# A long-convolution and mixer kernel: the matmuls of its last inverse stage put 16 apart, and its task order written out anew

## Chip, cores and metric

The kernel runs on one core of one Trainium2 chip, in one launch. The metric is the device time of an execution in microseconds (us), as the median of several runs. "Before" stands for the kernel without the change, "after" for the one with it.

## Reference

S = 2048 tokens, D = 640 channels, F = 1728. One sample, bfloat16 inputs. Cut to what matters:

```
mod = silu(c) @ w_mod                      # c is 1 x 640; six vectors sa, ca, ga, sb, cb, gb
q   = LN(x) * (1 + ca) + sa                # x = A_q
ks  = causal 4-tap convolution of k over the tokens, per channel
kv  = ks * v
y   = irfft(rfft(kv, 4096) * rfft(ssm_k, 4096))[:2048] + kv * ssm_D
x   = x + ga * (q * y)
h   = LN(x) * (1 + cb) + sb
g   = gelu(LN(h) @ w1)                     # 640 x 640
hs  = (g, its four quarters moved by +1, -1, +2, -2 tokens) @ w2
x1  = h + hs
h2  = gelu(LN(x1) @ w3) @ w4               # 640 x 1728, 1728 x 640
out = x + gb * (x1 + h2)
```

## The kernel before

**Tasks and their order.** The kernel builds 1056 numbered tasks with `add` (L91): for each a function that issues its instructions, the engines it may go to, what it reads and writes, and cost numbers. `run` (L121) then walks the string `ORDER` at the top of the file. A word such as `475P:20` is a task number, an engine letter (P TensorE, A ScalarE or ACT, D VectorE or DVE, G GpSimd or POOL, S SyncE or SP, which issues DMAs) and the PSUM places that the task takes, out of four places of two banks each. The functions are called in that order, so it fixes what each engine does one after the other, and on which engine a task with a choice lands. Within an engine nothing overtakes. The cost numbers are not read when the order is given.

**The convolution.** A transform of length 4096 is done as a product of small ones, 64 by 64. `to_slots` (L391) turns 32x32 blocks on DVE, `stage1` (L399, matmuls L408) and `stage2`/`stage2_half` (L416, L434; matmuls L425, L446) transform ssm_k and kv. ssm_D is added to the first tap of ssm_k (L461). `k_shift` (L472) does the four taps as matmuls with diagonal weights (L480). PSUM is read out by `evac` (L205; ACT is L208, DVE L210). `inverse1` (L623) multiplies the spectra on DVE (L633) and transforms back with matmuls L644 and L645, evacuated into the tile T01. `inverse2` (L673) is the last inverse stage: for tile A of 128 tokens it takes 32 matmuls (L685) of 32x32 weights (Hs) by 160 columns (Zb, in T01), one for each row group j4, column group cg and half cpp; the two halves of one j4 and cg add up in the same place of PSUM. It is called for the tile groups [0,1,2], [3,4], [5,6,7], [8,9,10], [11,12,13], [14,15]: the PE tasks 475, 478, 482, 485, 488, 491. Two evacuations of each (for 475: 476 and 477) write y_all.

**The modulation.** `mod_half` (L501) loads half of one of the six vectors' weights (400 KB), does five matmuls (L509) and stores a row of modv (L516 to L524). Tasks 428/429/430 and 431/432/433 are load, matmuls and evacuation of sb, 434 to 439 of gb. `x_load` (L538) brings x in pieces; 205 to 208 are the four pieces of its second half. `ln1_stats` (L549) and `make_q` (L613) make q; 444 and 447 are statistics of x tiles 11 and 13.

**The mixer.** `chain_a` (L756) forms q * y (L761) and adds it to x (L764); its tasks 520, 499, 540 are the first. `square_sum` (L752, ACT L753) and `ln_finish` (L720: a small first task on POOL or DVE, L726 to L731, and a second on POOL, L736 to L741) make the statistics of a layer norm. `chain_b` (L770; L775, L779, L780) makes h, `chain_c` (L808) normalizes it (`norm`, L605 to L610, or `normed`, L745) and transposes it with `turn` (L786): by PE and an evacuation (L796, L802/L804) for early groups, by a transposing DMA from SP (L789) for later ones. `mm_w1` (L831: L842 with gelu L844; L852 with gelu L858), `mm_w2` (L887: L897, evacuated by DVE at L904), `mm_w3` (L916: L931, gelu L935) and `mm_w4` (L939: L961, L952; DVE L984 to L990, stores L993) follow for groups of one or two tiles. The tasks 517, 536, 515, 556 are w1 of tiles 0, 1 and 2, 560/561 the first w2 and its evacuation, 600/598 w1 of the group of tiles 3 and 4, 649 to 652 normalization and transposing DMA of tiles 5 and 6, 661/659 their w1, 729 the L852 matmuls of tiles 7 and 8, fed by the transposing DMAs 718 and 720.

**Weights.** w1 (452) and w2 (453 to 457) are loaded into RG. w3 (494, L1020) and w4 (495 to 497) go where T01 was, so their loads wait until the last task of `inverse2` has read it.

Of the kernel before, what the change touches and what calls it, by code (L numbers as in the profile page):

```python
# [26 lines left out]
18D 19G 20D 21G 23D 24A 22D 27G 29D 36G 37G 30A 28D 50G 0S 2S 68G 69D 25A 31A 26G 84P:0 86P:1 88P:2 51D 53A 4S 72G 73D 106P:3 85A 87A 38G 104P:0 89A  # L27
107A 6S 3S 70G 71D 39G 40A 102P:1 103A 5S 74G 98P:2 99A 105D 8S 90P:3 91A 49G 118P:0 75D 110P:1 9S 119D 94P:2 32G 111A 95A 112P:3 113A 108P:0 109A
116P:1 114P:2 115A 1S 66D 67D 96P:3 117D 80P:0 82P:1 10S 122P:2 41G 42G 43G 44A 97A 52D 54A 45D 81A 83D 11S 123D 33G 78P:3 79A 100P:1 101D 76P:0 77A
136D 92P:2 34S 47S 120P:3 121D 93A 179P:1 55G 180A 46S 7S 193P:0 194A 35S 195P:2 196A 181P:1 147P:0 148A 182D 201S 141P:3 142D 139P:2 140A 143P:1  # L30
199P:0 175P:3 200A 48S 176A 144D 204S 185P:2 186D 161P:1 162A 65G 157P:0 158D 171P:3 172A 203S 165P:2 166D 191P:1 192A 167P:0 155P:3 156A 168D 169P:2
170A 177P:1 178D 189P:0 190A 151P:3 159P:2 160A 202S 152D 145P:1 146D 187P:0 188A 149P:3 150D 197P:2 198A 183P:1 184D 153P:0 154A 163P:3 164A 262P:2
173P:1 174A 12S 137P:0 138A 13S 214D 263A 126P:3 56G 264P:1 210D 254D 127D 57G 124P:0 125D 211D 58G 59G 60A 61G 62G 63G 265A 260P:2 215A 266P:1 267A
261A 14S 255D 64A 15S 128P:3 129D 258P:0 259A 270P:1 271A 130P:2 131D 256D 16S 212A 276P:0 277A 268P:1 269A 132P:3 134P:2 17S 133D 135D 257D 282P:0
209A 283A 223S 213G 224P:1 225A 220S 278P:3 226S 286P:2 287D 279A 221P:0 222A 272P:1 273A 274P:3 275A 227P:0 228D 469D 284P:1 463D 342S 285A 292P:2
293D 288P:0 289A 232S 233P:3 234D 290P:1 291D 466D 296P:2 297A 294P:0 295A 229S 230P:3 231D 343G 310P:1 302P:2 303A 311D 235S 460D 312P:3 313A 298P:0
299D 308P:1 309A 236P:2 237D 467D 300P:3 301A 306P:0 307D 280P:2 281A 316P:1 317D 252G 314P:3 315A 253S 304P:0 305D 318P:2 319A 248G 247G 320P:1 321A
241S 336P:3 340P:2 341A 337A 243G 240S 330P:0 331A 338P:1 339A 367G 251S 250G 239S 326P:2 322P:3 323A 464D 345D 344D 348P:0 349A 244G 346P:1 347A 352D
245S 249G 334P:3 238S 242S 351G 246G 335A 350S 353D 356P:0 357A 354P:1 366S 324P:3 325A 327D 359G 332P:2 333A 358S 360D 361D 362P:0 363A 368D 364P:3
328P:2 329A 355A 369D 370P:0 371A 365A 376D 375G 374S 372P:2 377D 378P:1 379A 380P:0 373A 381A 384D 217A 382S 383G 385D 388P:3 389A 391G 390S 393D  # L40
392D 386P:1 400D 387A 396P:2 397A 394P:0 398S 399G 401D 402P:3 425S 403A 404P:1 405A 408D 395A 426P:2 407G 406S 409D 416D 410P:3 415G 414S 417D 412P:1
431S 411A 465D 413A 461D 462D 427D 216G 420P:0 421D 418P:3 419A 470D 422S 423P:1 424D 471D 468D 218A 475P:20 476A 477D 520D 499D 434S 456S 500D 521D
540D 541D 543D 459G 472A 435P:3 436A 523D 473D 474D 432P:1 437S 438P:2 219G 501A 433A 512A 478P:03 439A 522A 502G 503G 428S 429P:1 430A 504D 505D 542A
491P:21 525D 479A 524G 507D 526D 528D 492A 506A 480A 568D 527A 545D 485P:02 487A 493A 486A 206S 544G 546D 547A 207S 508G 509D 510P:3 529G 511A 530D
531P:2 532A 482P:10 481G 569D 570A 548D 452S 571D 572D 574D 573A 458G 517P:3 518A 205S 513D 536P:2 533D 484D 549G 483A 550D 534D 575G 580D 581D 576D
455S 582D 457S 577D 578D 208S 514D 538P:3 584D 537A 535D 634D 635D 631D 539A 583A 488P:01 551P:2 552A 579A 585G 586D 515P:3 589D 632D 449D 489A 558P:2
516A 637D 559A 556P:0 557A 636A 453S 587P:3 633A 638G 590P:2 591A 490A 497S 588D 454S 560P:0 561D 562A 643D 600P:2 601A 639D 494S 563G 564G 598P:3
599A 498G 640D 641D 565D 566P:1 602P:0 605P:2 642A 644D 645D 647D 646A 648G 441D 649D 650S 567A 618P:3 446A 616P:1 603D 604A 651D 652S 620P:0 553A
496S 619A 606D 661P:2 617A 443D 607A 440D 608G 609G 613D 659P:3 610D 622P:1 444D 621A 554D 555D 699D 700D 662A 660A 614P:0 615A 611P:2 666P:3 667D
663P:0 612A 683P:2 623A 442G 664D 701A 668A 684A 665A 669G 670G 671A 679P:1 680A 677P:3 495S 674D 672P:0 675P:2 678A 592D 593D 595D 596D 597D 673A  # L50
594D 702D 624P:1 676A 749P:3 765D 766D 703D 704A 681P:0 747P:2 750A 682A 445G 653D 654D 655D 768D 769D 770A 705G 706G 625D 626D 767A 745P:3 685P:10
748A 743P:2 771G 707D 708D 711D 709D 710A 686P 712D 713D 772G 773D 777A 715G 714A 716G 717A 718S 774D 778D 779D 780A 775D 776A 744A 781D 719D 720S
687D 746A 447D 782G 783A 785D 448G 729P:1 730A 786S 727P:2 728A 784S 795P:3 721A 656D 693D 796A 657D 658D 831D 628S 832D 793P:0 450D 694D 724A 451G
722D 734P:1 723D 794A 834D 835D 836A 697S 787D 735D 731P:2 732D 737D 797P:3 798D 833A 751P:01 696S 688D 837G 838G 843D 800P:2 736A 725D 752P 844D 845D
733A 738G 741D 689S 839A 840D 841D 739A 801D 803D 627S 799A 847D 802A 740S 842A 846A 742S 753D 811P:3 812A 804G 807D 805A 815P:2 788D 809P:0 848G 851D
816A 813P:3 810A 849D 726D 852S 850S 855P:2 856A 808S 790D 853P:0 806S 873P:2 759D 854A 860P:1 791D 792D 891D 892D 789D 951D 952D 954D 857P:0 894D
895D 629S 893A 814A 861D 897D 896A 630S 898G 899D 900D 858D 863D 692S 875P:3 876A 871P:1 869P:3 691S 872A 754D 757S 870A 695S 817P:01 901D 874A
877P:32 818P 862A 859A 864G 903D 819D 758S 904D 905D 906A 865D 867D 868S 866S 907D 902A 908G 909D 911D 953A 955G 956D 957D 935P:0 936A 958D 960G 959A
961G 878P 690S 760D 825D 756S 912S 755S 519G 962D 826D 885D 910S 915P:0 916A 913P:1 914A 698S 820D 879D 931P:0 762S 963S 966P:2 967A 964P:1 917P:3
918D 920P:2 921D 822S 965A 969P:1 970D 932A 968G 1003P:0 933P:3 929P:2 827S 828S 919A 922A 923G 924G 927D 928S 764S 925D 926S 1004D 1005A 972P:1 973D  # L60
934A 971A 930A 937P:03 987P:2 761S 988A 981P:1 983P:2 763S 880D 884S 883S 824S 823S 821S 886D 887S 890S 939D 975D 974A 976G 985P:0 977A 979D 889S 982A
829S 938P 945D 882S 984A 978S 986A 980S 1016P:1 1014P:2 1010P:0 1017A 1011A 881S 1015A 1012P:3 1006G 1007G 1008D 1009S 989P:10 1013A 946D 830S 940D
941S 991D 947S 1032P:2 888S 992D 993S 996S 943S 1038P:3 990P 997D 1036P:1 1033A 1042D 1037A 1018P:20 995S 949S 1034P:1 1035A 1019P 944S 942S 998D
1002S 1000S 999S 950S 1020D 948S 1021D 1023S 1025S 1026D 1039A 994S 1027D 1001S 1024S 1040P:21 1022S 1043D 1030S 1028S 1031S 1044D 1045D 1047S 1048S
1046S 1029S 1049S 1041P 1050D 1051D 1055A 1052S 1053A 1054S
# [72 lines left out]
def kernel(  # L138
# [16 lines left out]
    add = pl.add  # L155
# [5 lines left out]
    T01 = mem.tile([P, 20480], BF, name="T01")  # L161
    R3 = mem.tile([P, 20480], BF, name="R3")
    R5 = mem.tile([P, 20560], BF, name="R5")
    RG = mem.tile([P, 8192], BF, name="RG")
# [67 lines left out]
    for b in range(ND):  # L232
        for dst, off, src, key in ((kT, 16, k_flat, "kT"), (vT, 0, v_flat, "vT")):
            add("SP", 3.0, lambda e, b=b, dst=dst, off=off, src=src: nc.sync.dma_start_transpose(dst[:, b, off:off + S], src[:, b * P:(b + 1) * P]),
                w=[(key, b, b + 1)], kb=524, rate=200.0)
# [100 lines left out]
    for kb in range(2):  # L336
# [9 lines left out]
        else:  # L346
# [3 lines left out]
            r=[wk[:3]], w=[wk], port=0.4)  # L350
# [83 lines left out]
    def stage2_half(h):  # L434
        for k0 in range(0, 32, 3):
            kn = min(3, 32 - k0)
            ps = Slot()

            def f(e, ps=ps, k0=k0, kn=kn, hh=h + 2):
                psv = pst(ps, name="ps_s2")[:, :, 0:480].rearrange("p g (k s) -> p g k s", k=3)  # L440
                for j in range(kn):
                    k = k0 + j
                    for cc in range(2):
                        for g in range(2):
                            p = slice(64 * g, 64 * g + 64)
                            nc.tensor.matmul(psv[:, g, j], lhsT=Gs[p, k, 64 - 64 * cc:192 - 64 * cc], rhs=T1h[h][p, cc * 32 + k],  # L446
                                             start=(cc == 0), stop=(cc == 1), tile_position=(64 * g, 0))
            t0 = add("PE", 0.145 * kn, f, r=[("T01", 10240 * h, 10240 * h + 10240), ("RG", 192 * k0, 192 * (k0 + kn))], alloc=ps, ni=8 * kn)
# [224 lines left out]
    def inverse2(tilesA):  # L673
# [3 lines left out]
        def f(e):  # L677
            for s in pss:
                pst(s, name="ps_i2")
            for a, A in enumerate(tilesA):  # L680
                for j4 in range(4):
                    for cg in range(4):
                        n1 = 4 * A + cg
                        for cpp in range(2):
# [35 lines left out]
    def ln_finish(li, t0, n, quick):  # L720
# [21 lines left out]
        add("POOL", 1.0 if quick else 1.3, f, port=-1, r=[("s2", 100 * li + t0, 100 * li + t0 + n), ("nm" + k, 0, 1)], w=[("ln" + k, 0, 1)])  # L742
# [346 lines left out]
```

## Time and profile before

| what | value |
|---|---|
| median of 3 runs | 302.70 us (302.69 to 303.25) |
| the profiled execution | 302.69 us |
| its span | 301.0 us |
| TensorE granted clock, mean | 0.97 |
| busy: PE, weight load, DVE, ACT, POOL | 271.0, 207.3, 220.8, 204.4, 108.9 us |
| first and last PE instruction | 8.43 and 296.2 us after the span's start |

The profile is that of one execution, taken by the hardware. Its page gives each engine's busy time, the span in forty equal slices (a digit is the busy tenths of a slice; PEclk is the TensorE clock that was granted, 9 being full), the DMA queues, the chain of work that ended last, and the costliest groups of instructions as "line, engine, operation, out<-in". Further views are cut from the same trace: busy time in chosen stretches, the chain in order of time, the timeline of one engine (in brackets the idle time ahead of a row and what ended it), and waits. "issue" means idle time in which an engine waited for nothing that the profile shows. PEld is the weight load of TensorE.

### The profile page before, as it was taken

What the parts mean: (1) busy time and instruction counts of PE and PEld (TensorE: products, weight loads), DVE (VectorE), ACT (ScalarE), POOL (GpSimd) and SP (SyncE); (2) the same over time, 40 slices, a digit from 0 to 9 for tenths busy, and PEclk for the clock granted to TensorE, in tenths of its full rate; (3) what the DMA queues carried; (4) which work ended last, traced back from release to release, by engine and by line L of the source; (5) the groups of instructions that cost most, each with busy time, mean ns of one, the idle gap of its engine ahead of it and who ended that gap; (6) DMA issues with size and microseconds to landing.
All of it is one profiled execution on the core that took longest, in us unless ns stands there. A gap on an engine that the chain in (4) does not pass through costs nothing.

```text
span 301.0 us, 7658 instructions
## 1 busy us (share of the span) xinstructions
PE 271.0 (90%) x3054; PEld 207.3 (69%) x3054; DVE 220.8 (73%) x446; ACT 204.4 (68%) x345; POOL 108.9 (36%) x238
## 2 busy tenths in 40 slices
PE   0899999979989576878999999999999999999993
PEld 0665655758888345756888787688867887887771
DVE  7999999979999979998659969983547343231343
ACT  4798999979999869998864679646451642604110
POOL 4967641451256646242345534310125120300000
PEclk9999999999999955799999999999999999999999
DMA  5998999998899940352900040234014112310121
GB/s 180 272 221 189 200 195 234 235 201 215 224 258 293 257 107 2 108 208 44 293 6 1 2 93 14 54 68 43 18 23 93 40 29 60 75 30 19 46 54 45
DMA packets 58179, 35.75 MB, mean 119 GB/s; under 512 B 39872, under 2 KB 54848, under 8 KB 58144
## 3 DMA queue, kind: packets, MB, share of 16 engines
q1 hardware_dynamic: 56944, 31.88, 45.2%
q0 software_dynamic: 1104, 3.34, 4.2%
q8 instruction: 24, 0.39, 0.5%
q14 instruction: 11, 0.09, 0.1%
q10 hardware_dynamic: 96, 0.04, 0.1%
HBM read 16.31 MB, written 2.62 MB: 63 GB/s over the span
## 4 chain that ended last, share of the span: by engine, by line
PE 71%; ACT 11%; DVE 6%; DMA 6%; issue 3%; POOL 1%; SPq 0%; ACTq 0%; DVEq 0%; POOLq 0%
PE ps_w L931 19%; PE ps_w L961 19%; PE ps_w L897 6%; PE ps_ksh L480 6%; PE ps_s L408 6%; PE ps_w L842 4%; ACT T L208 4%; ACT R L208 3%; PE ps_s L425 2%; PE ps_mod L509 2%; DMA RH<-in_w_mod_dram 2%; DMA Ra<-in_A_ssm_k_dram 2%; DVE R L780 1%; PE ps_i L644 1%; PE ps_s L446 1%
## 5 line engine op out<-in xcount | busy, mean ns | idle before, releaser
L931 PE MATMUL ps_w<-R,T 128*128 128x256 bf16 (+1 forms) x630 | 64.0, 261 | 0.0
L931 PEld LDWEIGHTS <-T 128*128 128x128 bf16 x630 | 55.7, 98 | 7.2 <-issue 1.1
L961 PE MATMUL ps_w<-T,R 128*128 128x320 bf16 x416 | 59.2, 299 | 0.0
L935 ACT ACTIVATE R<-ps_w 128x1024 bf16<-128x1024 f32 (+2 forms) x36 | 29.1, 828 | 42.1 <-PE ps_w L931 42.1
L961 PEld LDWEIGHTS <-R 128*128 128x128 bf16 x416 | 40.2, 98 | 15.8 <-ACT R L935 0.3
L208 ACT CAST T<-ps_s 128x1024 bf16<-128x1024 f32 x34 | 32.7, 1023 | 1.1 <-PE ps_s L408 1.1
L984 DVE TENSOR_TENSOR T<-ps_w,R 128x640 bf16<-128x640 f32 x15 | 12.3, 823 | 27.3 <-PE ps_w L961 14.0
L408 PE MATMUL ps_s<-F1bd,Rb 128*128 128x256 bf16 x160 | 22.9, 294 | 8.4 <-DVE Rb L395 8.4
L753 ACT ACTIVATE RG<-R 128x640 bf16<-128x640 bf16 x32 | 23.6, 736 | 10.2 <-DVE R L904 7.1
L208 ACT CAST R<-ps_s 128x640 bf16<-128x640 f32 (+1 forms) x36 | 26.7, 828 | 2.8 <-PE ps_s L446 1.9
L738 POOL TENSOR_TENSOR lnv<-stat,lnv 128x2 f32<-128x2 f32 x19 | 4.9, 256 | 62.6 <-ACT RG L753 33.0
L408 PEld LDWEIGHTS <-Rb 128*128 128x128 bf16 x160 | 16.4, 105 | 14.7 <-DVE Rb L395 8.8
L904 DVE SCALAR_TENSOR_TENSOR R<-ps_w,R 128x640 bf16<-128x640 f32 x16 | 13.1, 821 | 14.5 <-PE ps_w L897 14.5
L739 POOL TENSOR_TENSOR lnv<-lnv,mhalf 128x2 f32<-128x2 f32 (+1 forms) x29 | 22.3, 770 | 2.3
L897 PE MATMUL ps_w<-RG,R 128*128 128x320 bf16 x160 | 23.1, 299 | 0.0
L842 PE MATMUL ps_w<-R,RG 128*128 128x256 bf16 (+1 forms) x200 | 21.0, 267 | 0.3 <-ACT Rb L208 0.3
L644 PE MATMUL ps_i<-EA,Rb 128*128 128x128 bf16 x160 | 19.1, 219 | 1.2 <-ACT T L208 0.4
L645 PE MATMUL ps_i<-EB,Rb 128*128 128x128 bf16 x160 | 19.0, 219 | 0.5 <-DVE Rb L633 0.5
L897 PEld LDWEIGHTS <-R 128*128 128x128 bf16 x160 | 15.4, 98 | 6.0 <-issue 0.3
L842 PEld LDWEIGHTS <-RG 128*128 128x128 bf16 x200 | 18.2, 107 | 1.7 <-issue 0.4
L480 PE MATMUL ps_ksh<-R,RQ 128*128 128x512 bf16 x80 | 18.8, 380 | 0.0
L858 ACT ACTIVATE R<-ps_w1x 32x256 bf16<-32x256 f32 (+1 forms) x40 | 13.2, 330 | 7.8 <-PE ps_w1x L852 7.5
(179 smaller groups left out, 524.3 us busy)
## 6 DMA issues: line engine op xcount, KB each, us to landing
Ra<-in_A_ssm_k_dram SPq DMA_DIRECT2D x5, 512.0 KB, 5.6
Ra<-in_A_q_dram SPq DMA_DIRECT2D x8, 320.0 KB, 6.7
R<-in_w_mod_dram SPq DMA_DIRECT2D x6, 400.0 KB, 6.3
out_dram<-RH SPq DMA_DIRECT2D x60, 40.0 KB, 1.6
T<-in_B_w_dram SPq DMA_DIRECT2D x1, 2160.0 KB, 8.5
T<-in_B_w_dram SPq DMA_DIRECT2D x1, 2080.0 KB, 9.5
RH<-in_w_mod_dram SPq DMA_DIRECT2D x4, 400.0 KB, 4.3
RK<-R POOLq DMA_DIRECT2D x5, 256.0 KB, 4.5
```

Source lines behind the costliest of these rows:

```text
L208: nc.scalar.copy(dst, src(ps.tile))
L408: nc.tensor.matmul(psv[:, ml, :], lhsT=xL[:, s0:s0 + P], rhs=F1r, start=True, stop=True)
L480: nc.tensor.matmul(pt[:, i, :], lhsT=diagw[:, b, jj, :], rhs=kT[:, b, c0:c0 + 512], start=(jj == 0), stop=(jj == 3))
L644: nc.tensor.matmul(psv[:, w, :], lhsT=Av[:, r_, :, g_], rhs=EAf, start=True, stop=False)
L645: nc.tensor.matmul(psv[:, w, :], lhsT=Bv[:, r_, :, g_], rhs=EBf, start=False, stop=True)
L739: nc.gpsimd.tensor_tensor(rs, rs, mhalf[:, 0:n], ALU.pow)
L753: add("ACT", 0.74, lambda e: nc.scalar.activation(junk, src, ACT.Square, scale=float(D) ** -0.5, accum_out=stat[:, li, 1, t:t + 1]), r=[sk ...
L842: nc.tensor.matmul(pt[:, fb, 0:cw], lhsT=w1_sb[:, b, 160 * fb:160 * fb + P], rhs=hT[:, b, 0:cw], start=(b == 0), stop=(b == ND - 1))
L897: nc.tensor.matmul(pt[:, hf, 0:320], lhsT=gsf[:, fb, c0:c0 + P], rhs=w2_sb[:, fb, 320 * hf:320 * hf + 320], start=(fb == 0), stop=(fb == 4))
L931: nc.tensor.matmul(pt[:, fl, 0:cw], lhsT=w3_sb[:, b, fb * P:(fb + 1) * P], rhs=xT[:, b, 0:cw], start=(b == 0), stop=(b == ND - 1))
L935: nc.scalar.activation(g3[g % 2][:, f0:f0 + fn, 0:cw], ps.tile[:, 0:fn, 0:cw], ACT.Gelu_apprx_tanh)
L961: nc.tensor.matmul(bank(i, hf), lhsT=gg[:, fb, i * P:(i + 1) * P], rhs=w4_sb[:, fb, 320 * hf:320 * hf + 320], start=(fb == 0 and i == 0), ...
```

## The change

Three things change.

1. The string `ORDER` is replaced as a whole. The PE tasks are the same 241. The tasks with a choice of engine change like this: evacuations (L206 to L210) 9 from ACT to DVE and 9 from DVE to ACT; normalizations (L606 to L610) 13 from DVE to ACT and 6 from ACT to DVE; evacuations of PE transposes (L799 to L804) 5 from ACT to DVE and 1 back; layer-norm statistics of x 2 from DVE to ACT and 1 back; the first task of `ln_finish` 7 from DVE to POOL and 4 from POOL to DVE; one L461 from POOL to DVE; DMA copies of the tables and half spectra 7 from SP to POOL and 4 from POOL to SP. Tasks in all: DVE 308 and then 302, ACT 249 and 253, POOL 99 and 104, SP 159 and 156. The cut below shows the part around the last inverse stage.
2. In `inverse2` the loop over the two halves, cpp, is moved outside the loops over j4 and cg. The two matmuls that add into one place of PSUM are 16 matmuls apart; they were neighbours.
3. Cost numbers of `stage2_half` and `ln_finish` change, and an unused default argument goes.

```diff
 ORDER = """
...
-431S 411A 465D 413A ... 218A 475P:20 476A 477D 520D 499D 434S 456S 500D 521D
-540D 541D 543D 459G 472A 435P:3 436A 523D 473D 474D 432P:1 437S 438P:2 219G 501A 433A 512A 478P:03 439A 522A 502G 503G 428S 429P:1 430A 504D 505D 542A
-491P:21 525D 479A 524G 507D 526D 528D 492A 506A 480A 568D 527A 545D 485P:02 ...
...
+427D 452S 410P:1 411A 412P:2 413A 420P:0 421D 418P:1 419A 422S 423P:3 456S 461D 470D 424D 468D 462D 218A 475P:20 477D 476A 520D 459G 454S 499D 500D
+471D 521D 472A 540D 434S 219G 523D 541D 543D 437S 438P:1 439A 512A 435P:3 428S 429P:2 430A 431S 432P:0 501A 522A 433A 436A 525D 502G 504D 457S 478P:12
+480A 503G 524G 526D 505D 473D 491P:03 545D 542A 544G 507D 553A 492A 527A 474D 546D 479A 571D 568D 485P:20 ...
...
 """
@@ stage2_half
-            def f(e, ps=ps, k0=k0, kn=kn, hh=h + 2):
+            def f(e, ps=ps, k0=k0, kn=kn):
...
-            t0 = add("PE", 0.145 * kn, f, ...
+            t0 = add("PE", 0.17 * kn, f, ...
@@ inverse2
             for a, A in enumerate(tilesA):
-                for j4 in range(4):
-                    for cg in range(4):
-                        n1 = 4 * A + cg
-                        for cpp in range(2):
+                for cpp in range(2):
+                    for j4 in range(4):
+                        for cg in range(4):
+                            n1 = 4 * A + cg
                             nc.tensor.matmul(pss[j4 // 2].tile[32 * cg:32 * cg + 32, j4 % 2, a * 160:(a + 1) * 160],
                                              lhsT=Hs[32 * j4:32 * j4 + 32, n1, cpp, :],
                                              rhs=Zb[32 * j4:32 * j4 + 32, cpp * 64 + n1, :, :],
                                              start=(cpp == 0), stop=(cpp == 1), tile_position=(32 * j4, 32 * cg))
@@ ln_finish
-        add("POOL", 1.0 if quick else 1.3, f, ...
+        add("POOL", 0.8 if quick else 1.1, f, ...
```

The loads that stand on SP's queue from 425 (w_mod) to 496 run, before: 425, 431, 422, 434, 456, 437, 428, 206, 207, 452, 205, 455, 457, 208, 453, 497, 454, 494, then the transposing DMAs 650 and 652, 496, 495. After: 425, 452, 422, 456, 454, 434, 437, 428, 431, 457, 208, 207, 453, 455, 206, 494, 205, 497, 652, 650, 495, 496.

## The prediction, made before the changed kernel was run

> **What bounds the kernel now.** I read the page first: the engines' shares, the forty slices, the chain. The profiled execution took 302.69 us, the median of the three runs is 302.70, so the sum below is made against 302.69 and stands for the median too. The span is 301.0; 1.69 us lie around it and I leave them alone. About 0.2% (0.6 us) is what a measurement of this kernel can tell from no change.
>
> ```profile
> span 301.0 us, 7658 instructions
> ...
> PE 271.0 (90%) x3054; PEld 207.3 (69%) x3054; DVE 220.8 (73%) x446; ACT 204.4 (68%) x345; POOL 108.9 (36%) x238
> ...
> PE   0899999979989576878999999999999999999993
> ...
> PEclk9999999999999955799999999999999999999999
> ```
>
> TensorE holds the end, but the PE row has a dent: slices 14 to 19 (about 98 to 143 us), and the granted clock falls there. So I asked for the busy time by stage, in stretches that begin where the final inverse stage begins and where PE is full for good:
>
> ```profile
> 60.00:98.20 38.20, 34.05 (x606) 29.53 (x605) 36.07 (x39) 35.66 (x43) 16.38 (x27) 1.00 0.94 238
> 98.20:143.13 44.93, 32.88 (x752) 25.07 (x753) 40.10 (x108) 39.74 (x88) 20.01 (x51) 0.81 0.44 120
> 143.13:296.30 153.17, 153.09 (x1318) 120.64 (x1318) 87.53 (x214) 76.36 (x140) 38.62 (x105) 1.00 0.24 53
> ```
>
> Columns after the length: busy PE, weight load, DVE, ACT, POOL, clock, DMA share, GB/s. From 143.13 PE is busy 153.09 of 153.17 us: nothing but its own sum counts. From 98.20 to 143.13 PE is idle 12 us, DVE and ACT are busy 40.1 and 39.7 of 44.9: they bound that stretch, by the order in which they take their tasks. The chain of waits there:
>
> ```profile
> 98.20 1.20 PE ps_i L685 x88
> 99.40 2.14 PE ps_mod L509 x15
> 101.54 0.55 PE ps_i L685 x22
> 102.09 3.70 issue
> 105.79 0.97 PE ps_i L685 x41
> 106.76 1.46 PE ps_mod L509 x5
> 108.24 0.43 ACT modv L524
> 108.77 0.90 DVE R L780 x2
> ...
> 140.39 2.60 DMA R<-RK
> 143.00 0.14 issue
> 143.13 0.71 PE ps_w1x L852 x5
> ```
>
> Two things are to be seen. First, PE stops for 3.70 us at 102.09 inside the second L685 task, with nothing to wait for ("issue"). The trace's records of the queue "instruction" (24 fetches of 16 KB, one for each 256 PE instructions) say why: fetches began at 91.09 and 102.89 us, after 1785 and 2241 PE instructions had started, 456 apart where 240 to 310 is usual. The late one took 1.30 us; PE went on 1.6 us after it. The loads issued from 93.3 to 98.7 (w_mod, x, w1, w2) keep all DMA engines full at 220 to 370 GB/s just then. Second, 429, the mod row queued behind that task on PE, comes 3.7 us late, and DVE waits for it:
>
> ```profile
> 108.77 0.89 DVE L780 SCALAR_TENSOR_TENSOR R<-R,lnv,modv 128x640 bf16<-128x640 bf16 x1 [1.74 <-ACT modv L524]
> ```
>
> So the point that sets the end is X, the start of task 661 (143.13 now): the time after is X plus PE's remaining sum (153.1) plus the tail (4.8).
>
> **Part 2, the inner order of L685.** Nothing is added: 512 matmuls and 512 weight loads as before. The timeline shows task 475 (96 matmuls, three tiles) from 98.20 to 99.33, 0.376 us a tile at full clock: 16 tiles, 6.0 us. Bounds: at most the stream itself, 160 columns at the 2.35 columns per ns of L931's 128x256 (109 ns apart) over 16 array positions and 32 matmuls, 0.14 us a tile; the quickest 32 matmuls of the trace took 0.21 us. So the stage may lose 0 to 2.6 us of PE time (3.8 at the extreme), but PE has 12 us of idle time here, and only 475 is waited for directly (its evacuations 476 and 477 start chain_a): at most 3 x 0.17 = 0.5 us. The other way, if 16 open accumulations were dearer than neighbours, nothing in the trace excludes +0.5. I take -0.2 on the path. Of the fetch stall it takes nothing: a quicker task runs dry sooner and waits for the same fetch.
>
> One rule speaks against this part. "TensorE: Matmul & The Clock Gate" in the Trainium skill, Part 3, "The mechanism", says that a weight load overlaps matmuls in flight only when its row group differs. The new order still takes four column groups of one row group in a row, and by that rule three of four loads stay unoverlapped and the gain is nothing: the sum would be 0.2 us worse.
>
> **Part 3, cost numbers and an unused default.** They feed no instruction: the order is read from the string. 0.
>
> **Part 1, the order.** PE has the same 241 tasks; 60-odd tasks elsewhere change engine (18 evacuations and 19 normalizations among them). I summed each engine's old durations along the new order.
>
> *To 60 us:* DVE's running sums stay within 0.2 us at the first transposes and PE's order is nearly the same; the k and v transposes for block 4 come before 2. 0. *To 98.2:* ACT's tasks ahead of 476 sum to 99.08 instead of 98.40 us (+0.68), PE's wait at 60.65 for w_mod has 0.44 more PE work ahead of it. ACT is 93% busy there, so I put chain_a 0.9 later (row 520: 100.78 to 101.65). **+0.9, less the 0.2 above.**
>
> *Mod rows.* The new order records all four of that time (438, 435, 429, 432) right after 475, ahead of the second L685 task. Their loads, by the same rates and the new queue order, land at 96.5 to 101.5, and all four lie before instruction 2241. The fetch stall stays (I estimate 105.2 plus or minus 1, against 105.79, since the same loads are in flight) but what is behind it now are L685 tiles that DVE needs only later. **-1.74** on DVE and -2.67 on ACT (its wait on L509). If cover is gone (a mod load lands 3 us later), they come back in full.
>
> *DVE to the first w2 evacuation (561).* From 520 to 561 DVE's own tasks sum to 24.96 before and 24.19 after, -0.77: seven small statistics tasks go to POOL. Each such pair of rows occupies DVE for 0.3 to 0.4 us with its gaps (104.59 to 105.22 for two), not the 0.2 its durations say: -0.77 to -1.9, I take **-1.2**. POOL is busy 20 of 45 us here and has room; its rows are about 0.26 us (L738), and where a normalization waits for them (L741: 0.46, 0.28, 0.65) the waits grow, up to +0.5 each for the three; I take **+0.3**. So 561 starts at 131.13 + 0.7 - 1.74 - 1.2 + 0.3, about 129.2.
>
> *From there to X.* The last normalization before the transposing DMA ends at 140.05 now. After: task 444 (1.1 us, x statistics) and 563 (0.33) go ahead, one L904 (0.82) goes behind: +0.6; the wait of 0.65 ahead of 138.50 is filled by 444: -0.65; 0.28 at 132.24 partly: -0.2. Two transposes in the other sequence and the 2.60 of the DMA are unchanged. **-0.2.** Sum at X: 0.7 - 1.74 - 1.2 + 0.3 - 0.2 = -2.1; ACT's tasks up to there are +0.26 in sum, against its -2.67, so it doesn't take over. X about 141.0.
>
> *The full tail.* PE's sum after X is the same, but PE takes 729 (w1 of a later group) 2.2 us earlier in its sequence: sum 133.96 instead of 136.14. Its operand comes by transposing DMAs (issued 173.78, landed about 176.4, used 177.13: 0.7 in hand). DVE's sequence is also drawn forward, not wholly: I estimate a wait of 0 to 1.5, and take **+0.5**. The other transposed operands sit within 0.6 us of their old place. Stores at the end: the last two are the same tasks. 0.
>
> Sum: 302.69 - 2.1 + 0.5 = **301.1 us**. The bounds: 302.69 - 2.1 - 0.3 (L685) - 0.7 (statistics) + 0 = about 299.1 to 299.6, and with the dear ends (+0.7 L685, +0.7, +1.0) 303.
>
> **Rivals.**
> *The gain is larger (298.7).* L685 runs at 0.21 us a tile (0.3 more at 475), and the fetch comes at its usual 256 instructions, since PE reaches its mark before the loads fill the engines; then the 3.7 us of idle go, and with them the low clock after it (0.52 and 0.57 from 105.4 to 120.4). Two w1 tasks that stand in the chain there cost 2.01 and 2.34 us, 1.12 each at full clock: 2.1 more. For: clock 0.81 in the stretch. Against: the loads are issued at the same time.
>
> *Given back in the tail (302.7).* The gain at X meets 729 and its neighbours at the full 1.5, then the next group at 1.2 less. No change.
>
> *The next fetch meets the w3 load: slower.* In before the fetch for the twelfth block began at 123.47, the 2.16 MB w3 load (L1020) was issued at 123.9 and its packets ran from 125.5 to 131.6 at over 400 GB/s: the fetch was ahead by 0.4 us. In the new order the load waits for the same last L685 task, and the fetch mark (about instruction 2944) lies in that very task. If the fetch falls behind, PE runs dry near instruction 3265 (task 600, w1) until the load ends, about 130.5, plus 1.3 to 1.6 for the fetch; from 600 to 661 are 11.9 us in before (131.27 to 143.13), so X is 143.4 to 144, and with +0.5 in the tail the time 303.5 to 304.3, say **304.0**. It decides when the load's first packets come ahead of the fetch. "Runtime: NRT & Kernel Launch", section "Instruction fetch mechanics", says that crossing a block is mostly hidden; by it this rival is nothing. The 3.70 us at 102.09 in this trace disagree.
>
> *Something queued is late (304 to 306).* One x piece (205) is now behind the w3 load on SP's queue; DVE's task 444 needs it at about 134 and stands ahead of 649 and the transposes. It lands at 131 to 132 by the 400 GB/s above; above 134 DVE waits, each us on X.
>
> **How the numbers follow.** Forecast 0.42 (faster nearly whole: 0.40, same 0.02); larger gain 0.13; given back 0.13 (same 0.07, slower 0.06); fetch behind w3 0.20 and late x piece 0.12 (both slower). Faster 0.53, same 0.09, slower 0.38. The range leaves out half of the late piece and some of the larger gain: 298.2 to 304.8; the forecast's own is 299.1 to 302.1.
>
> **What would show it.** Right: L524 done before 106 and no wait of L780 over 1 us; X (first L852 row after the last PE gap) at 140 to 142; PE idle under 1 us after it. Wrong: PE idle "issue" of more than 1 us past 125; the L780 wait back; X at 143 or later; a DMA wait of PE near X + 31.6. For part 2: a tile of L685 under 0.3 us at clock 1.00; 0.376 would say it does nothing.

## The result and the profile after

The changed kernel took 306.84 us (median of 4 runs, 306.06 to 307.53), the kernel before 302.98 (4 runs, 302.69 to 303.45): a ratio of 1.0125, 95% interval 1.0089 to 1.0162. It is slower by about 1.25%, where I forecast 301.1. The profiled execution of after took 306.06 us with a span of 304.3.

The page of after, the lines that answer to those of before:

```profile
span 304.3 us, 7652 instructions
...
PE 268.7 (88%) x3054; PEld 205.5 (68%) x3054; DVE 218.0 (72%) x432; ACT 210.1 (69%) x352; POOL 113.3 (37%) x251
...
PE   0899999998989637877999899998999998999993
...
PEclk9999999999999857799999999999999999999998
```

The dent between about 98 and 143 us is still there, and three single 8s have come into the run of 9s behind it. So I cut the stretch behind X, which runs to the last matmul, out of both kernels. Columns: busy PE, weight load, DVE, ACT, POOL, then clock, DMA share, GB/s. Before:

```profile
143.13:296.22 153.09, 153.09 (x1318) 120.64 (x1318) 87.49 (x213) 76.36 (x140) 38.62 (x105) 1.00 0.24 53
```

After:

```profile
142.09:299.25 157.16, 153.66 (x1318) 120.44 (x1318) 84.62 (x206) 82.56 (x150) 40.31 (x113) 1.00 0.23 51
```

X came 1.04 us earlier (142.09, not 143.13), and the same 1318 matmuls then needed 157.16 us instead of 153.09: 4.07 more, of which PE was busy 0.57 and idle 3.50. The sum: -1.04 + 4.07 = 3.03 at the last matmul, 0.27 in the tail, 0.07 around the span, 3.37 in all, which is 306.06 - 302.69. The timeline of PE from X on shows where the idle time stands (in brackets the idle time ahead of the row and what ended it):

```profile
142.09 0.71 PE L852 MATMUL ps_w1x<-R,RG 128*128 128x256 bf16 x5 [1.19 <-DMA R<-RK]
...
175.44 0.71 PE L852 MATMUL ps_w1x<-R,RG 128*128 128x256 bf16 x5 [1.38 <-DVE RQ L618]
...
208.21 3.44 PE L931 MATMUL ps_w<-R,T 128*128 128x256 bf16 x30 [1.29 <-DMA R<-RH]
...
257.15 7.80 PE L931 MATMUL ps_w<-R,T 128*128 128x256 bf16 x70 [0.76 <-DMA R<-RH]
```

The row at 142.09 is X itself. Behind it PE waits three times: at task 729 (1.38), 875 (1.29) and 987 (0.76), 3.43 us together. All three are the first matmuls on an operand that a transposing DMA of SP brings. The first is put down to DVE L618, which ended at 175.37; but 720, the DMA, was issued at 172.71, and with the 2.6 us that its kind takes elsewhere it landed at 175.3 too, and 729 needs it and not the L618 row. In before no row of PE behind X has such a bracket. Of the 1.38, part belongs to this one execution: the transposing DMA ahead of 720 on SP, 718, kept SP for 2.47 us here, where 1.2 is usual.

### The profile page after: what moved, and what is told of

Same layout as the page of the kernel before. It is cut to its first block, busy times and chain, and to the rows that moved or that the text cites. A ratio compares the mean times of both kernels' runs of the same rounds, so it can differ in the third digit from the quotient of the medians.

```text
span 304.3 us, 7652 instructions
## 1 busy us (share of the span) xinstructions
PE 268.7 (88%) x3054; PEld 205.5 (68%) x3054; DVE 218.0 (72%) x432; ACT 210.1 (69%) x352; POOL 113.3 (37%) x251
## 4 chain that ended last, share of the span: by engine, by line
PE 55%; DMA 13%; DVE 9%; ACT 8%; issue 6%; POOL 4%; SPq 2%; ACTq 0%; DVEq 0%; POOLq 0%
PE ps_w L931 18%; PE ps_w L961 15%; PE ps_ksh L480 5%; PE ps_w L897 4%; PE ps_s L408 4%; PE ps_w L842 3%; ACT R L208 3%; DMA R<-in_w_mod_dram 2%; DMA RG<-R 2%; ACT RG L753 2%; DMA R<-RH 2%; DMA Rb<-R 2%; DMA RK<-R 1%; POOL lnv L739 1%; DMA RH<-RK 1%
## 5 line engine op out<-in xcount | busy, mean ns | idle before, releaser
L753 ACT ACTIVATE RG<-R 128x640 bf16<-128x640 bf16 x32 | 23.5, 735 | 13.2 <-DVE R L780 9.1
L739 POOL TENSOR_TENSOR lnv<-lnv,mhalf 128x2 f32<-128x2 f32 (+1 forms) x29 | 23.6, 815 | 2.3
L726 POOL TENSOR_SCALAR lnv<-stat 128x2 f32<-128x2 f32 (+1 forms) x14 | 4.9, 349 | 45.2 <-DVE Ra L764 18.0
L738 POOL TENSOR_TENSOR lnv<-stat,lnv 128x2 f32<-128x2 f32 x19 | 4.0, 209 | 39.5 <-ACT RG L753 26.0
```

The source lines that it names most:

```text
L739: nc.gpsimd.tensor_tensor(rs, rs, mhalf[:, 0:n], ALU.pow)
L753: add("ACT", 0.74, lambda e: nc.scalar.activation(junk, src, ACT.Square, scale=float(D) ** -0.5, accum_out=stat[:, li, 1, t:t + 1]), r=[sk ...
```

## The experiments

The theory after the result: **the loss lies behind X, in the order of the tasks that feed PE there**. Rivals: the loops of L685 cost it; the part ahead of X leaves work behind that comes due later. The runs of the kernel before beside each group spread from 300.6 to 306.5 us, with medians of 302.69, 303.78 and 302.25, so ratios are what to compare.

Each run has one profile, of one of its executions; the time given is the median of all of them.

**a_oldloop**: after's order, before's loops.

```diff
-                for cpp in range(2):
-                    for j4 in range(4):
-                        for cg in range(4):
-                            n1 = 4 * A + cg
+                for j4 in range(4):
+                    for cg in range(4):
+                        n1 = 4 * A + cg
+                        for cpp in range(2):
```

> After's order with before's loops in the last inverse stage (part 2 undone). Theory tail: the loss is three PE waits after X (1.38 us ahead of 729, 1.29 ahead of 875, 0.76 ahead of 987 in the trace of after), which the loops don't touch; task 475 is about 0.2 us slower again, so X is 0 to 0.3 later and the time 306 to 307.5, the waits still there. Rival loop: the matmuls 16 apart are dear (open accumulations, weights), so 303.

Measured: 305.31 us, ratio 1.0069 (1.0036 to 1.0103). X at 141.63, waits of 0.85, 0.45, 1.53 and 0.82 us behind it (729, 793, 875, 987), last matmul at 299.08 against 299.25 in after. The time is below the 306 to 307.5 that I expected, but the waits stay, 3.72 us of idle time behind X in sum; the loops are not the loss.

**b_newloop**: before's order, after's loops (the diff above, the other way round).

> Before's order with after's loops in the last inverse stage (part 2 alone). Theory tail: 302.4 to 303.2, X within 0.3 us of 143.1, no PE wait after it. Rival loop: 305 to 307.

Measured: 302.16 us, ratio 0.9979 (0.9948 to 1.0011), X 142.32, waits of PE behind X 0.07 in sum. Part 2 alone costs nothing; a gain of some tenths is possible and not settled: X is 0.8 us earlier than in the profile of before, but so much it moves between executions of one order too (below). What it does to the task itself is plain. Task 475 before, and in b_newloop:

```profile
98.20 1.20 PE L685 MATMUL ps_i<-T,RH 32*32 32x160 bf16 x96 [0.42 <-ACT T L208]
```

```profile
96.78 1.02 PE L685 MATMUL ps_i<-T,RH 32*32 32x160 bf16 x96 [0.42 <-ACT T L208]
```

Every kernel here with the old loops shows 1.20 for it, every one with the new loops 1.02 or 1.03.

**head_a_tail_b**: after's order to task 659, then before's. **head_b_tail_a**: the other way round. Both have after's loops.

```diff
 ORDER: words up to 659P from one order,
+       then the words of the other that have not come yet, in its sequence; PSUM places dealt anew
```

> After's order up to the w1 of tiles 5 and 6 (task 659), then what is left in before's relative order, PSUM places dealt out anew. Theory tail: X as in after (142.1), PE without waits over 0.3 us behind it, so 153.1 us later its end: 1 us faster than before, 301.5 to 302.3. Rival head: the loss is made before X and carried on (tasks left behind), 305 to 307.

> Before's order up to task 659, then what is left in after's relative order. Theory tail: X as in before (143.1) and waits of 2 to 4 us ahead of 729, 875 and 987 behind it: 305 to 307.5. Rival head: 302.5 to 303.5.

Measured: head_a_tail_b 305.76, ratio 1.0069 (1.0032 to 1.0107); head_b_tail_a 309.72, ratio 1.0203 (1.0147 to 1.0259). Both are above what the theory gave. The profile of head_a_tail_b is of an execution of 303.66 us, the second fastest of its twelve, so what the slower ones lost more is not seen. Both have a wait that the splice made: tasks that one order has early and the other late (446 on ACT, 554, 444 and 447 on DVE) fell in between and held up the PE transposes at 147 to 149 us, 1.48 us in the one and 2.74 in the other. Behind that, head_a_tail_b has no bracket of PE over 0.4; head_b_tail_a has 1.12 at 179.59, 1.02 at 211.98 and 0.55 at 260.71, the three places again. Beside its 2.74 the granted clock fell to 0.50 for 3.4 us, and PE's busy time behind X is 154.87 us (153.66 in after): that is lost to the splice too. So the splice was mended in a second round, beside the changed kernel itself.

**after_again**: the changed kernel, unedited.

> The changed kernel itself, beside the others and with a second profile. All theories: 305.5 to 307.5. Theory tail: the same three PE waits behind X (ahead of 729, 875, 987), 3 to 4 us in all; if the 2.47 us that the transposing DMA 718 kept SP (1.2 to 1.3 is usual) was an accident of one execution, the wait ahead of 729 falls to 0.2 to 0.8 here.

Measured: 306.38, ratio 1.0116 (1.0067 to 1.0165). X is 1.4 us later than in the first profile (143.49), yet the last matmul stands at 299.26, with waits of 0.80 (729), 0.49 (793) and 0.64 (987). 718 kept SP for 1.21 us here, and the wait at 729 fell as expected; 875 doesn't wait in this execution. The stretch behind X is 155.77 us, 2.69 more than in before, of which 2.06 is idle. Which tasks wait, and how long, thus differs between executions; X itself is 0.36 later than in before here.

**head_a_tail_b2**: the splice with 446 behind 701 on ACT and 449 behind 664 on DVE.

```diff
-659P:2 449D 446A 496S ... 701A ... 664D
+659P:2 496S ... 701A 446A ... 664D 449D
```

> The spliced order (after's up to task 659, then before's) without the 1.48 us that the splice itself cost at 147.39 (446 on ACT ahead of 660): 446 and 449 are put behind the turns. Theory tail: X 141.9, no wait over 0.3 behind it, profile 301 to 302, median 301.5 to 303. Rival: something in after's head that doesn't show as a wait of PE behind X keeps it at 305 to 306.

Measured: 303.47, ratio 0.9998 (0.9968 to 1.0028): the loss is gone. The stretch from X to the last matmul, and what PE waited for from 142 us on (the first row is X; columns: us in total, times, longest):

```profile
141.74:295.83 154.09, 153.53 (x1318) 120.61 (x1318) 86.25 (x213) 78.56 (x146) 38.82 (x109) 1.00 0.22 53
```

```profile
PE ps_w1x L852 <- DMA R<-RK: 1.2, 1, 1.2
PE ps_tr L796 <- ACT R L844: 0.3, 1, 0.3
PE ps_w L931 <- DMA R<-RH: 0.2, 1, 0.2
```

Idle behind X falls from 3.50 to 0.56 us. The head is after's and the loops are after's; only the order behind task 659 differs, with the PSUM places dealt anew there and, for 29 tasks, the engine that before had chosen. The changed kernel in the same group has 1.0116, and the two intervals do not meet (1.0067 the low end of the one, 1.0028 the high end of the other). This is the run that shows the cause, the order behind 659. The sequence, the places and the engines in it are not separated; the waits that went were for operands that the sequence makes late. The median is a little above the 301.5 to 303 that I expected; 0.46 us of that lies outside the profiled span (2.15 us against 1.69 in before), and nothing here says why.

**a_tailfix**: edits behind X in after. The expectation names three. The first, 729 one place later, changed nothing on PE, since no other PE task stands between its old place and its new one. The others:

```diff
-847G 842A 846A ... 848G 851D ... 799A 852S 802A 804G 807D ... 805D 850S ... 808S ... 806S
+799A 802A 804G 847G 842A 846A ... 848G 807D 805D 851D ... 808S 806S 852S 850S
-881S ... 926S 927A 928S
+926S 927A 928S 881S
```

> After with three edits behind X: PE task 729 one place later; the square sums 799 and 802, their statistics 804, normalizations 807 and 805 and transposing DMAs 808 and 806 ahead of those of the other group; the store 881 behind the transposing DMA 928. Theory tail: the waits ahead of 875 and 987 go to under 0.3 us each and that ahead of 729 to under 0.3; 3 us less than after: 303 to 304.5. Rival: PE's sum rules and the waits only move to other tasks: 305.5 to 307.

Measured: 306.14, ratio 1.0088 (1.0056 to 1.0119): a miss. The waits at 875 and 987 are gone, but a new one of 1.10 us stands at 853 (its PSUM place is freed by a later gelu), and 729 keeps 1.09:

```profile
PE ps_w L842 <- ACT R L935: 1.1, 1, 1.1
PE ps_w1x L852 <- DMA R<-RK: 1.1, 1, 1.1
PE ps_w L842 <- DMA R<-RK: 0.2, 1, 0.2
```

**a_all**: the same, and 649 right behind 651 on DVE, and the w_mod load 431 ahead of 422 on SP.

> The three edits behind X, and two ahead of it: normalization 649 right behind 651 (ahead of the w2 evacuation 606) and the w_mod load 431 three loads earlier on SP. Theory tail and head: PE's 1.9 to 2.1 us wait ahead of 432 (about 101 to 103) goes, X at 140.2 to 141.3, no waits behind X: 301.5 to 303. Rival: X stays at 142 since DVE and ACT are full: 303 to 304.5.

Measured: 306.12, ratio 1.0077 (1.004 to 1.0113). X 143.76; PE's waits for w_mod loads did not go but split (0.63, 0.67, 1.38), and X did not move forward. Behind X the waits are 0.80 (729), 0.54 (793) and 1.12 (853). Missed on both counts. That one load put earlier makes another late would fit the DMA engines, which were full there (busy share 1.11 by the profile between 96 and 102 us), but was not tried by itself.

**a_two**: after with the w3 task 743 ahead of 729, and the store 881 behind 928.

```diff
-729P:3 773D ... 746A 727P:0 ... 743P:1
+743P:3 773D ... 746A 729P:0 744A 727P:1
```

> After with two edits behind X: the w3 task 743 goes ahead of the w1 task 729 on PE (where before has it), and the store 881 behind the transposing DMA 928 on SP. Theory tail: the waits ahead of 729 and 987 fall under 0.3 us, that ahead of 875 stays at 0.8 to 1.5; 1 to 2 us less than after, a ratio of 1.004 to 1.008 to before. Rival: other operands come late in their place (727, 793): ratio 1.011 as after.

Measured: 309.39, ratio 1.0212 (1.0171 to 1.0254). 729 and 987 no longer wait, 875 still does, and a new wait of 3.92 us stands at 183.66, where w2 needs the gelu of the w1 task 727 that I had pushed back:

```profile
PE ps_w L897 <- ACT R L844: 3.9, 1, 3.9
PE ps_w L931 <- DMA R<-RH: 1.3, 1, 1.3
```

That wait cost more than its length. The granted clock was 0.50 in the 3.4 us behind it, and PE's busy time behind X is 155.06 us, 1.40 more than in after. The same stands beside the other two waits over 2 us at X or behind it, 2.74 in head_b_tail_a and 2.11 in b_xlate; the other eleven profiles have no wait over 1.9 us there and no fall of the clock from X to the last matmul. The rows (columns as above, the clock third from the end) for a_two, head_b_tail_a and b_xlate:

```profile
183.66:187.00 3.34, 3.34 (x13) 1.93 (x14) 1.60 (x4) 0.86 (x3) 0.00 (x0) 0.50 0.25 49
```

```profile
147.90:151.30 3.40, 2.66 (x17) 1.97 (x18) 1.14 (x4) 0.94 (x3) 1.12 (x3) 0.50 0.43 146
```

```profile
143.20:146.50 3.30, 3.08 (x15) 2.24 (x16) 2.77 (x9) 2.18 (x7) 2.55 (x6) 0.50 0.82 238
```

So the rival on record won in kind, and worse than its 1.011: one edit frees one wait and makes the next. None of these three sets of edits mended the order.

**b_mod429**: ahead of X: before, with the mod row 429 ahead of the second L685 task.

```diff
-437S 438P:2 ... 512A 478P:03 439A 522A 502G 503G 428S 429P:1 430A
+437S 428S 438P:2 ... 512A 429P:1 478P:03 439A 430A 522A 502G 503G
```

> Before, with one edit: the mod row 429 (load 428, evacuation 430) ahead of the second L685 task 478, as after has it. Theory: the DVE wait of 1.74 on L524 goes to under 0.5, but the statistics of POOL (L739, L741), which DVE then reaches early, keep half of it: their waits grow from 1.39 to about 2.2 in all; X 0.5 to 1.2 earlier, 301.5 to 302.5. Rival: the whole 1.74 arrives at X: 300.9 to 301.3. Rival: nothing, 302.5 to 303.

Measured: 302.00, ratio 0.9995 (0.9952 to 1.0037). DVE's waits over 0.2 us between 98 and 142 us in it:

```profile
125.94 0.80 DVE L610 TENSOR_SCALAR RK<-R,lnv 128x640 bf16<-128x640 bf16 x2 [0.88 <-POOL lnv L741]
130.70 0.84 DVE L610 TENSOR_SCALAR R<-Ra,lnv 128x640 bf16<-128x640 bf16 x2 [0.49 <-POOL lnv L741]
133.40 0.55 DVE L748 TENSOR_SCALAR RH<-R,lnv 128x640 bf16<-128x640 bf16 x1 [0.46 <-POOL lnv L739]
137.50 0.45 DVE L610 TENSOR_SCALAR RK<-R,lnv 128x640 bf16<-128x640 bf16 x1 [0.65 <-POOL lnv L741]
```

The 1.74 on L524 is gone; the waits for POOL's statistics grew from 1.39 (0.46, 0.28, 0.65) to 2.48. From task 475 to X it is 44.76 us, against 44.93 in before: 0.17 of the 1.74 arrived in this pair of executions, less than the half that I had expected. The next run shows that one pair is not enough to say so.

**b_mod429_new**: the same with after's loops.

> The same order as b_mod429 with after's loops in the last inverse stage: the two single parts that looked useful, together. Theory: 0.2 to 0.8 us below b_mod429, ratio 0.992 to 0.998 to before. Rival, the loops are worth nothing: as b_mod429.

Measured: 301.76, ratio 0.9981 (0.9937 to 1.0026), X 141.69. Against b_newloop, which lacks only the moved row, the stretch from 475 to X is 43.88 us instead of 45.54: 1.66 less, where a wait of 2.24 on L524 went and POOL's grew from 1.39 to 1.80. So one pair of profiles has a tenth of the stall arrive and the other most of it. The best median of all, but its interval takes in no change: a version that beats both kernels clearly was not found.

**b_xlate**: before, with the x loads behind the w3 load.

```diff
-206S ... 207S ... 205S ... 208S ... 494S
+494S 205S 206S 207S 208S
-449D ... 440D
+440D 449D
```

> Before, with the four x loads (205 to 208, 1.28 MB) moved behind the w3 load on SP, and 449, which reads them, moved behind 440 on DVE (1.1 us of DVE work goes from ahead of X to behind it). Theory A, the PE instruction fetch waits behind the loads in flight: the fetch that began at 102.89 begins at 97 to 100, the idle of 3.70 us inside the second L685 task falls under 1, so does the 1.74 of DVE: 300 to 302. Theory B, the fetch is started by PE's own place in the program: it stays at 101 to 103 and the idle at 3 to 4.5: 301 to 303.

Measured: 304.32, ratio 1.0062 (1.0015 to 1.0109). The fetch began at 102.20 (102.89 in before) and the idle time on "issue" was 2.33 us (3.70). It does not tell the theories apart: w1 and w2 moved up into the place of the x loads, so from 96 to 102 us DMA moved 1.9 MB (1.7 in before), and the fetch began just when that had drained; that fits a fetch behind what was queued, but PE had also run dry by then, which fits the other. b_newloop speaks against the other: PE ran dry at 100.64 there, and the fetch began only at 102.36. The loss has another cause. X is only 0.29 us later, but PE's busy time behind it is 154.72 us (153.09 in before), with the clock at 0.50 from 143.1 on, beside the wait of 2.11 us ahead of X (see a_two). What delayed X's operand is DVE: in this order its statistics wait for x.

```profile
137.80 0.89 DVE L554 BATCH_NORM_STATS2 ln_st<-Ra 128x6 f32<-128x320 bf16 x2 [2.41 <-DMA Ra<-in_A_q_dram]
```

## Why the prediction was wrong, step by step

**Part 2: right in size.** I took -0.2 on the path for L685; task 475 went from 1.20 to 1.02 us. From first to last start that is 0.264 us a tile instead of 0.326. (By the prediction's own measure, to the start of the next row, it is 0.32 in b_newloop instead of 0.376, not the under 0.3 that I had set as the sign.) I had weighed a rule of the Trainium skill against it ("TensorE: Matmul & The Clock Gate", Part 3, "The mechanism": weight loads overlap matmuls in flight only in another row group). I applied it wrongly: before takes eight loads of one row group in a row and the new order four, so by the rule itself the new order should rather gain. Nor does the trace show the rule in either order: a load is some 87 ns long there, and 32 of them with their matmuls pass in 264 or 326 ns, so loads do overlap within one row group. Why the new order is quicker was not tried.

**Start of chain_a: sign wrong, and not the order's doing.** I put it 0.7 later; task 475 began at 97.46, 0.74 earlier. Over the other kernels it begins at 97.1 to 99.3 with after's head and at 96.8 to 98.4 with before's. The order hardly sets it.

**The wait of 1.74 on L524: right.** Task 430 on ACT was done at 102.2, and no wait on L524 is left. The fetch stall stayed, as I wrote, and fell on L685 tiles (2.83 us of "issue" at 108.04, ended at 110.87 and not at about 105.2).

**POOL's statistics, "+0.3": mis-sized.** This is the first step that failed. DVE's waits for POOL in before:

```profile
127.80 0.80 DVE L610 TENSOR_SCALAR RK<-R,lnv 128x640 bf16<-128x640 bf16 x2 [0.46 <-POOL lnv L741]
132.24 0.84 DVE L610 TENSOR_SCALAR R<-Ra,lnv 128x640 bf16<-128x640 bf16 x2 [0.28 <-POOL lnv L741]
138.50 0.45 DVE L610 TENSOR_SCALAR RK<-R,lnv 128x640 bf16<-128x640 bf16 x1 [0.65 <-POOL lnv L741]
```

DVE's waits between 98 and 143 us in after:

```profile
106.88 0.88 DVE L780 SCALAR_TENSOR_TENSOR R<-R,lnv,modv 128x640 bf16<-128x640 bf16 x1 [0.45 <-POOL lnv L739]
115.56 0.45 DVE L748 TENSOR_SCALAR RK<-R,lnv 128x640 bf16<-128x640 bf16 x1 [0.45 <-POOL lnv L739]
118.75 0.80 DVE L610 TENSOR_SCALAR R<-Ra,lnv 128x640 bf16<-128x640 bf16 x2 [0.40 <-POOL lnv L741]
125.57 0.80 DVE L610 TENSOR_SCALAR RK<-R,lnv 128x640 bf16<-128x640 bf16 x2 [0.87 <-POOL lnv L741]
129.35 0.82 DVE L904 SCALAR_TENSOR_TENSOR R<-ps_w,R 128x640 bf16<-128x640 f32 x1 [0.91 <-PE ps_w L897]
133.25 0.45 DVE L748 TENSOR_SCALAR RH<-R,lnv 128x640 bf16<-128x640 bf16 x1 [0.45 <-POOL lnv L739]
137.24 0.54 DVE L610 TENSOR_SCALAR RK<-R,lnv 128x640 bf16<-128x640 bf16 x1 [0.24 <-POOL lnv L741]
```

Six waits for POOL, 2.86 us (1.39 in before), and 0.91 for w2: 1.5 + 0.9 where I had 0.3. I asked what each engine still had to do and not how long a tile takes through DVE, ACT (L753), POOL (L738 to L741) and back; a DVE that arrives earlier waits there. In b_mod429 the waits for POOL grew in the same way. Task 561 did start at 129.35 (its row above), where I had 129.2, but by luck: 475 came 1.4 us earlier than I had put it, and these waits used that up. So the stretch from 475 to X fell from 44.93 to 44.63 us, 0.3, where my steps without the start came to 2.8; X was -1.04, mostly the earlier start, not -2.1.

Even that gain is not shown. Six executions with after's head and loops (after, after_again, head_a_tail_b, head_a_tail_b2, a_tailfix, a_two) take 44.12 to 45.54 us from 475 to X and have X at 141.7 to 143.5; three with before's head (before, b_newloop, head_b_tail_a) take 44.93 to 45.54 and have X at 142.3 to 143.1. Ahead of X the new order gained nothing that stands out of this spread.

**The full tail, "+0.5": the step that turned the sign.** It measured +4.07 (+2.69 in after_again), 3.50 of it idle time of PE. Here I had priced one wait, at 729, by PE's place in its sequence and 0.7 us in hand (0 to 1.5 us; it came to 1.38 and 0.80), and wrote that the other transposed operands "sit within 0.6 us of their old place". That was PE's sequence alone. What feeds it had moved the other way: the transposing DMA 806 was issued 2.32 us later than in before (204.23 against 201.91) and 928 8.85 us later (254.40 against 245.54). The chain of waits ahead of 987 shows how:

```profile
248.39 0.42 SPq L993
248.81 0.04 issue
248.85 3.19 DMA out_dram<-RH
252.04 0.03 issue
252.07 0.05 DVEq L990
252.12 0.04 issue
252.16 0.50 DVE RH L990
252.67 0.02 issue
252.68 0.32 SPq L993
253.00 0.05 issue
253.05 0.03 SPq L789
253.08 0.03 issue
253.11 1.20 SPq L789
```

Stores that SP gets to late (L993) keep an output buffer, DVE waits for it at L990, the next store (881) waits for that DVE row, and the transposing DMA (L789) stands behind the store on SP; a_tailfix and a_two, which take 881 out of its way, have no wait at 987. The wait at 875 comes by ACT: the square sums 799 and 802 stand behind two others that are not ready, and ACT is idle from 190.38 to 196.38, when the first of those two starts:

```profile
196.38 0.74 ACT L753 ACTIVATE RG<-R 128x640 bf16<-128x640 bf16 x1 [6.00 <-DVE R L780]
```

With 799 and 802 moved ahead of them (a_tailfix) the wait at 875 is gone. For these two the order on SP and on ACT is at fault, not any engine's load.

**The rivals.** "Given back in the tail" comes nearest, by waits of the tail that I had priced at no more than the gain; they took more than X had gained. "The fetch meets the w3 load" did not happen: in after the fetch began at 122.17, next to the load's issue at 121.85, and PE had no "issue" wait over 1 us past 125. "Something queued is late" did not either: 444 ran at 135.88 without a wait for x. And the larger gain did not come: PE waited for a fetch again, and the granted clock from 98.20 to X is 0.81 as in before.

**The sums.** The dear ends that I named add up to 303.5 from the forecast, not 303, and the cheap ones to 299.6. And I took 0.6 us for what a measurement can tell from no change; single executions of before spread by 6 us over 68 runs.

**Open.** What the 0.57 us of added busy PE time behind X are was not found: the granted clock is 1.00 in both, and head_a_tail_b2, with before's tail, still has 0.44 of it. Nor did I find which few words of the tail would mend after's order: three sets of edits moved the waits.

## What to carry to other kernels

Where an engine is full, the price of a new order is not in its own sequence but in how late each operand now comes: walk every queue that feeds it (the transposing DMAs, the stores ahead of them on the same queue, the square sums ahead of the statistics) as carefully as the engine itself. A stall that goes ahead of a chain through three engines is worth what that chain leaves of it, and one pair of profiles may not tell how much: here 0.17 of 1.74 us in one pair, 1.66 of 2.24 in another. And an order in which all queues were placed against each other has little slack: taking single tasks out of it moved the waits, and only the whole stretch put back removed them.

## What was not expected of the hardware

Fetches of PE instructions began, in the stretch behind 170 us, mostly 150 to 180 PE instructions past a multiple of 256; in the L685 stage they came up to 449 past one, and PE stood on "issue" for 0.8 to 4.5 us at a time in every profile here, near instruction 2240 in before's order and 2490 in after's. The Trainium skill, "Runtime: NRT & Kernel Launch", section "Instruction fetch mechanics", calls the crossing mostly hidden; that holds for the rest of this kernel (no wait on "issue" shows on PE elsewhere in before and after) and not for its L685 stage, which takes 80 to 94 matmuls a microsecond. The time of the same kernel spread by 6 us (300.6 to 306.5 for before in 68 runs of three groups), and the last inverse stage began anywhere from 96.8 to 99.3 us. A transposing DMA from SBUF that mostly lands in 2.6 to 2.7 us took 3.84 when issued at 204.23 in after, and the same one 3.92 in before.
